# Gated linear attention feeding a maxout feed-forward layer: 16-bit transposition of the results, decay sums by TensorE, copies on either engine, and a new written order

## The chip, the core and the metric

The kernel runs on one core of a Trainium2 chip. The metric is device time in microseconds (us) of one execution. A core has five instruction queues that run side by side and meet only through semaphores: TensorE (PE), which multiplies matrices and writes to the accumulator memory PSUM; VectorE (DVE); ScalarE (ACT); GpSimd (POOL); and SyncE (SP), which here only issues DMA transfers. Each queue works strictly in the order in which its instructions were written, so an instruction that waits holds up everything behind it on its engine.

## The reference

The first half is a recurrence per batch and head, with a state matrix of 48 by 48; the second is a feed-forward layer over all 3072 tokens.

```python
# q, k, v, alpha: (4 batches, 8 heads, 768 steps, 48), alpha in 0.8 to 1.0
for t in range(S):
    state = alpha[:, :, t, :, None] * state + einsum('bhd,bhe->bhde', k[:, :, t], v[:, :, t])
    y[:, :, t] = einsum('bhd,bhde->bhe', q[:, :, t], state)
x = y.transpose(0, 2, 1, 3).reshape(3072, 384)
h = maximum(maximum(x @ w1, x @ w2), x @ w3)      # 384 -> 768
out = h @ w_out                                    # 768 -> 384
```

## The kernel before

**Tiling.** Time is cut into three chunks of 256 steps per batch, which makes twelve chunks n = 0 to 11 (chunk n is time block n // 4 of batch n % 4). A partition holds two neighbouring steps of a chunk, called r = 0 and r = 1, and 64 partitions make one half i of the chunk. The heads go in two groups of four, so a chunk has two units u = 2n and 2n + 1.

**Attention, per chunk.** `decay` takes logarithms of alpha on ACT (L355) and of the product of two neighbours (L350 for the product, on POOL or DVE; L360 for the logarithm). In `prep`, PE sums the logarithms with a triangular matrix (L425) to get the decay of the odd step, and DVE subtracts one logarithm from that, in PSUM, to get the even step (L429, step "L0"). ACT takes both exponentials (L434, tiles `ep` and `en`), and q and k are multiplied with them on POOL or DVE (L439, tile `qk`). PE turns q and k (L464, step "tp"), always two units together from chunk 2 on; DVE copies the turned q and k out of PSUM (L478, tile `qkT`, 128 x 1024 of 16 bits); PE forms the scores (L490, step "A"); DVE masks them (L498, tile `LA`). `state` sums k and v of the chunk (L522, step "pp") and carries the state on (L399, L411). `output` adds the part of the old state (L555) and the masked scores times v (L577) in PSUM. The result is scaled to 16 bits (tile `xb`, L258 on ACT or L260 on DVE), turned on PE into token order (L598, step "xp"), and copied out (L254, tile `xT`).

The turning is a matmul with `order`, a 0/1 matrix that puts the even steps and the odd ones back in sequence; it writes 32-bit numbers:

```python
live[xk] = bank(xk, [P, NFT, P], FP32)
for ft in range(NFT):
    nc.tensor.matmul(live[xk][:, ft, :], xb[:, :, ft], order, start=True, stop=True)
```

**Feed-forward, per chunk.** The maximum of three products is written with differences: w2 - w1 and w3 - w1 are formed once by DVE in place (L307, tile `wcat`, two halves g = 0, 1 of three column pieces each). Six groups of six matmuls per chunk give the two hidden products (L621, step "gp"); the first half passes a ReLU (L630 on ACT, L632 on DVE), the second a maximum with the first (L637, DVE). What w1 does by itself is folded into one matrix `past` = w1 times w_out (L320 transposes w1, L254 copies it to `w1T`, L333 multiplies). An output block of 128 tokens then takes three matmuls with `past` (L654) and six with w_out (L657); ACT or DVE copies it (L254, tile `ob`) and SP stores it (L673).

**Order.** Nothing is scheduled when the kernel is built. Every piece of work is a step with a number; the text `ORDER` lists all step numbers in program order, each with the letter of the engine that runs it (P, V, A, G, S for PE, DVE, ACT, POOL, SP) and the PSUM banks that it takes. For example `28P0` is step 28 on PE in bank 0. So ORDER fixes each engine's queue, the choice of engine where a step may run on two, and the bank each result lies in. There are eight banks. SP issues all loads of q, k, v and alpha (L273), five chunks deep, and the stores; POOL issues the four weight loads (L287, L290), which therefore stand in POOL's queue between its products.

The functions that the change touches, and what calls them:

Of the kernel before, what the change touches and what calls it, by code (L numbers as in the profile page):

```python
# [10 lines left out]
FP32 = mybir.dt.float32  # L11
FP16 = mybir.dt.float16
# [14 lines left out]
0S 3S 53S 6S 7S 5S 2S 1S 11V 12A 8V 13A 4S 10A 28P0 9A 54S 14P1 29V 17P2 57V 55S 30A 18V 31A 56S  # L27
59A 33V 100S 58A 60P3 75P4 19A 102S 63P5 76V 34A 101S 32V 61A 20A 103S 64V 35P6 15A 22V 145S 21V
207S 23A 36V 24P2 148S 65A 16V 40P01 146S 25V 77A 78A 147S 67G 26P6 41V 66A 275S 37P2 39G 79V 343S
42V 209S 38V 80G 208S 277S 74G 82P4 68V 69A 278S 70P2 62G 86G 210S 83V 45P0 276S 71V 81G 27V 104G  # L30
72P4 87P23 73V 46P6 50A 89V 84P4 47A 88V 85V 106A 92P7 48P0 105A 411S 49V 93P2 51P6 94V 97A 110P4
90V 98P5 111V 117P0 107P7 44V 197P2 108A 91V 52A 195P7 189V 112A 95P3 99A 118V 257P6 113A 190V 120A
261P5 258V 96A 196A 191V 325P4 122V 262A 265P3 43V 115G 119A 199P6 266A 329P7 131G 326A 121V 200A
114V 194V 124P0 116A 193V 333P5 125V 123A 330A 128V 126P3 149G 334A 132P67 127V 129P0 150A 331P5
109G 151A 198A 134V 335P3 133V 130V 162P4 137P6 267P2 163V 152P0 263P1 332V 165A 153A 192V 164A
138P5 154G 336V 259P0 211G 139A 136V 155P4 205P3 156V 213A 168G 142V 157A 203P5 161A 135V 260V 158A
166G 220P6 212A 327P7 264V 204A 143P4 268V 159G 214P0 140P1 144A 201P5 221V 141A 167V 215A 206A
227P2 393P4 160V 202A 217G 228V 169P0 279G 328V 229A 176P35 230A 173V 269P7 219G 223A 178V 347G
281A 170V 394A 177V 222A 282P2 174P0 180V 283A 225G 171P3 270A 337P6 175V 280A 232G 611S 172V 345S
288P2 181P7 224G 338A 295P0 272P1 348A 296V 231G 289V 297A 179V 349A 182P6 285V 298A 287V 234P3  # L40
291A 216V 273V 286G 340P5 183A 218G 238V 186A 274S 300G 290A 235V 344S 363P0 239P6 677S 341A 233G
364V 397P1 294A 240V 346S 226G 187P2 479S 350P3 299G 398A 399P4 545S 351A 236P5 188A 293G 400V 414S
241P71 301A 184P3 342S 401P2 242V 185A 284G 243V 413S 237V 366A 403P4 245G 402A 412S 244G 356P7
465P3 292G 480S 247V 309P25 357V 481S 466A 467P6 404V 415G 365A 548S 246V 249P3 359A 248P4 339S
310V 302P0 358A 368G 468V 546S 417A 250P 311V 416A 482S 469P7 353G 306V 313G 251A 271S 312G 461P6
303V 254A 614S 360G 470A 315V 418P2 307P3 547S 314V 462A 304P0 252P7 308V 367G 419A 255P5 463P6
253A 256A 361G 316P2 305V 317P7 362A 395P3 369G 471P4 464V 421G 352G 431P5 318P 355G 472V 354G
370P0 322A 423G 535P6 374V 319A 483G 424P4 527P7 396V 536A 549G 531P2 371V 528A 377P36 425V 430G
551A 375P0 408P7 378V 532A 379V 380G 432V 485A 381G 376V 434A 426A 533P3 436G 433A 382V 492P2 427A
372P0 383V 422G 552P5 484A 320P4 476P6 429G 493V 534V 495A 428G 321A 373V 494A 537P3 477A 435G  # L50
323P4 616A 529P2 409V 324A 538V 385P6 553A 558P0 384P1 550A 486P7 438P4 530V 487A 386P 489G 488V
437G 559V 499P3 565P7 387A 473P2 420V 390V 497G 561A 500V 439V 615G 501A 388P1 405P6 474A 566V 389A
442V 502A 491V 560A 391P2 504G 440P4 392A 593P1 441V 555G 490G 597P3 594A 445P02 568A 443P4 598A
659P1 447V 446V 617A 449G 444V 599P3 406A 496G 407S 663P0 681V 475S 661P6 664A 563V 678S 539P4 660A
498G 600V 410S 683A 564G 612S 567A 448V 618P5 679S 562G 665P0 450V 540V 680S 667P1 451V 505G 541S
666V 631P3 452P7 668A 595P4 613S 632V 619A 503V 624P2 634A 453P0 684P1 513P5 596V 621G 633A 570G
454P 685A 682A 515V 506P3 662V 458A 571G 669P1 455A 625V 635G 514V 627A 459P0 601P6 507V 626A 569G
460A 456P7 670V 542P5 602A 510V 554G 557G 628G 511P0 543A 508P2 579P6 512V 457A 630G 544S 572P4
556G 725P7 516V 509V 687G 729P0 629G 726A 603P1 730A 689G 580V 518P7 731P2 517V 581V 636G 690P3
573V 674P0 691V 582G 576V 637G 519P6 732V 583G 638P4 675A 693A 604V 520P 676S 697P0 622V 727P2 521A  # L60
524V 692A 733P1 698V 639V 699A 522P7 605P6 523A 728V 701G 734A 642V 688G 577P2 606A 574P4 585P7
578V 700A 607S 525P1 671P6 702G 526A 478S 575V 623G 584P0 703G 735P1 672A 696A 694G 673S 586P 736V
645P2 620G 643P3 686G 640P5 646V 608P1 647V 587V 641V 751P2 609A 644V 590A 740P0 610S 591P5 743P6
592V 588P1 649V 747P7 589A 648V 752V 741A 650P3 651P4 765P5 742S 695V 652P 744V 704P0 653A 711P2
656A 769P6 712V 766A 713V 657P3 705V 654P4 715G 770A 737P2 708V 658A 748A 714V 655A 706P5 709P0
717P3 707V 779P7 749P4 780A 710V 787P5 716P6 750V 763P7 718P 753P0 745P1 754V 789P4 719V 761P0 746V
783P6 722V 762A 767P1 764V 723P3 755P0 724V 738V 784V 720P7 758P3 721V 797P2 759V 771P6 788V 760S
805P7 756V 772V 785P3 757S 798V 739S 801P5 806V 781P0 768V 803P6 802V 773P2 790V 804V 799P7 782V
807P1 786V 776P5 800V 808V 791P4 774V 777V 775S 778S 813P6 792V 809P0 793S 817P3 814P 810P 815V
818P 794P7 811A 816S 812S 819V 820S 795A 796S  # L70
# [44 lines left out]
def kernel(  # L115
# [41 lines left out]
    c16_np = np.concatenate([np.kron(both, trimid), halves], axis=1).astype(np.float16)  # L157
# [9 lines left out]
    c16 = sb.tile([P, P + 4], FP16, name="c16")  # L167
    d16 = sb.tile([P, 4 * P], FP16, name="d16")
    c32 = sb.tile([P, 3], FP32, name="c32")
    tri, hsel = c16[:, :P], c16[:, P:]  # L170
# [79 lines left out]
    TB = 2  # L250
    WAFTER = {2: (0,), 4: (1,), 7: (2,), 11: (3,)}
# [164 lines left out]
    def prep(u):  # L416
# [6 lines left out]
        def cums(eng):  # L423
            live[Lk] = bank(Lk, [P, HH, 2, D], FP32)
            nc.tensor.matmul(live[Lk][:, :, 1, :], tri, la[:, 0, hs, :D], start=True, stop=True)  # L425

        plan.step("Lp", "PE", u, cums, banks=[Lk], reads=[("la", n % 3, hh, 0)], writes=[Lk])
        plan.step("L0", "DVE", u,
                  lambda eng: nc.vector.tensor_sub(live[Lk][:, :, 0, :], live[Lk][:, :, 1, :],  # L429
                                                   la[:, 1, hs, :D]),  # L430
                  reads=[Lk, ("la", n % 3, hh, 1)], writes=[(Lk, 0)])
# [39 lines left out]
        for v in units:  # L471
            attend(v, tk)


    def attend(u, tk):
        qkT, LA, Ak = qkTs[u % NT_], LAs[u % NT_], ("A", u)
        plan.step("qkT", "DVE", u,
                  lambda eng: nc.vector.tensor_copy(  # L478
                      out=qkT.rearrange("p i w j t -> p i (w j t)"), in_=live["tp", u]),
                  reads=[tk], writes=[("qkT", u % NT_)])  # L480

        def scores(eng):
            live[Ak] = banks2(Ak, FP32)
# [246 lines left out]
```

## Time and profile before

| | us |
|---|---|
| median of 3 runs | 152.37 |
| lowest and highest of them | 151.62, 154.77 |
| the profiled execution | 150.92 |
| its span, from first to last instruction | 149.2 |
| PE busy, matmuls | 130.2 |
| DVE busy | 121.8 |
| ACT busy | 80.7 |
| POOL busy | 71.8 |

The busy times are sums over the whole span, and a matmul's busy time has a modelled end, so they tell which engine is much used and not yet which one sets the end. For that the profile has the span in 40 slices with the tenths that each engine was busy, and the chain of work that ended last, followed back from the last instruction. A group's row gives line, engine, operation, tiles, shape and count, then busy time and mean duration of one in ns, then how long the engine stood idle just before it and what ended that. Durations of one matmul (200 to 330 ns) are longer than the distance at which they follow each other; the distances come from the timeline.

Input loads keep the DMA near 260 GB/s in the first 78 us; the granted clock of PE was full throughout.

### The profile page before, as it was taken

Reading aid. Unit: us, or ns where it says so; the run is one execution under the profiler, and the core shown is the slowest. Engines: PE = TensorE matmul, PEld = TensorE weight load, DVE = VectorE, ACT = ScalarE, POOL = GpSimd, SP = SyncE. Lnnn points to the kernel's source line nnn. Section 1 sums busy time; section 2 is a strip of 40 time slices with the busy share of each in tenths; the row PEclk is TensorE's granted clock in tenths of the full one; section 3 lists DMA queues with packets and bytes.
Section 4 is the critical chain, followed back from the end, with each engine's and each line's share of the span. In section 5 each row is a group of like instructions: output and inputs, shape, how many; then the busy total and the mean of one; then the engine's idle time right before and its main releaser. Section 6 shows DMA issues by size and latency. Waiting matters only on the chain.

```text
span 149.2 us, 5617 instructions
## 1 busy us (share of the span) xinstructions
PE 130.2 (87%) x2389; PEld 101.2 (68%) x2389; DVE 121.8 (82%) x231; ACT 80.7 (54%) x182; POOL 71.8 (48%) x114
## 2 busy tenths in 40 slices
PE   0136587689999999999999999999999999999991
PEld 0025475468676678887687879778678788787670
DVE  6489996789999979998896899699698785889720
ACT  3565156687896887957877759328522720100011
POOL 8105900430959897999977577994730100000000
PEclk9999999999999999999999999999999999999999
DMA  5999999999999999999996199701211100031223
GB/s 112 266 262 263 252 216 213 278 234 252 277 260 265 258 266 281 254 253 280 276 256 166 57 258 284 203 2 59 105 57 53 57 4 0 4 110 48 81 101 134
DMA packets 54728, 26.34 MB, mean 177 GB/s; under 512 B 50736, under 2 KB 54320, under 8 KB 54704
## 3 DMA queue, kind: packets, MB, share of 16 engines
q1 hardware_dynamic: 53584, 23.60, 63.3%
q0 software_dynamic: 832, 2.36, 8.1%
q8 instruction: 18, 0.29, 0.9%
q10 hardware_dynamic: 288, 0.04, 0.3%
q14 instruction: 6, 0.05, 0.1%
HBM read 23.63 MB, written 4.72 MB: 190 GB/s over the span
## 4 chain that ended last, share of the span: by engine, by line
PE 65%; DMA 10%; POOL 6%; DVE 5%; ACT 4%; SPq 4%; issue 3%; POOLq 0%; DVEq 0%
PE psum L621 26%; PE psum L657 15%; PE psum L654 8%; DMA wcat<-in_moe_w_dram 6%; SPq L273 4%; DMA qn<-in_q_dram 4%; POOL qk L439 3%; PE psum L490 3%; PE psum L577 3%; PE psum L464 3%; PE psum L598 2%; PE psum L333 2%; PE psum L555 2%; PE psum L522 2%; POOL Z L399 1%
## 5 line engine op out<-in xcount | busy, mean ns | idle before, releaser
L621 PE MATMUL psum<-xT,wcat 128*128 128x256 f16 x432 | 54.3, 273 | 2.1 <-DVE wcat L307 2.1
L621 PEld LDWEIGHTS <-wcat 128*128 128x128 f16 x432 | 39.9, 98 | 8.4 <-DVE wcat L307 2.8
L498 DVE TENSOR_TENSOR LA<-psum,d 128x1024 f16<-128x1024 f32 x24 | 28.7, 1217 | 3.7 <-PE psum L490 2.8
L657 PE MATMUL psum<-wo,hT 128*128 128x384 f16 (+1 forms) x150 | 27.5, 320 | 0.0
L637 DVE TENSOR_TENSOR hT<-psum,hT 128x512 f16<-128x512 f32 x36 | 23.7, 680 | 2.9 <-PE psum L621 2.6
L439 POOL TENSOR_TENSOR qk<-qn,ep 128x384 f16<-128x384 f32 x18 | 18.3, 1026 | 11.4 <-DMA qn<-in_q_dram 8.6
L630 ACT ACTIVATE hT<-psum 128x512 f16<-128x512 f32 x28 | 16.4, 601 | 13.6 <-PE psum L621 13.2
L254 ACT COPY ob<-psum 128x384 f32<-128x384 f32 x14 | 6.7, 481 | 27.9 <-PE psum L657 27.9
L657 PEld LDWEIGHTS <-hT 128*128 128x128 f16 x150 | 14.5, 98 | 8.9
L439 POOL TENSOR_TENSOR qk<-kn,en 128x384 f16<-128x384 f32 x16 | 15.9, 998 | 9.4 <-ACT en L434 8.9
L478 DVE COPY qkT<-psum 128x1024 f16<-128x1024 f16 x24 | 16.0, 683 | 1.3 <-PE psum L464 1.1
L654 PE MATMUL psum<-past,xT 128*128 128x384 f16 (+1 forms) x75 | 15.9, 321 | 0.0
L258 ACT ACTIVATE xb<-psum,c 128x384 f16<-128x384 f32 x17 | 9.2, 581 | 8.7 <-PE psum L577 8.6
L434 ACT ACTIVATE en<-psum 128x384 f32<-128x384 f32 x24 | 11.5, 492 | 2.0 <-DVE psum L429 2.0
L464 PE MATMUL psum<-d,qk 64*128 64x64 f16 x384 | 8.8, 198 | 4.1 <-POOL qk L439 2.1
L434 ACT ACTIVATE ep<-psum 128x384 f32<-128x384 f32 x24 | 11.6, 492 | 0.9 <-DVE psum L429 0.6
L254 ACT CAST xT<-psum 128x384 f16<-128x384 f32 x20 | 9.4, 482 | 3.0 <-PE psum L598 2.7
L350 POOL TENSOR_TENSOR aa<-an 128x384 f32<-128x384 f32 x9 | 8.9, 998 | 4.3 <-DMA an<-in_alpha_dram 4.1
L425 PE MATMUL psum<-la,c 128*128 128x192 f16 x24 | 6.1, 272 | 5.5 <-ACT la L360 5.5
L464 PEld LDWEIGHTS <-qk 64*128 64x128 f16 x384 | 7.1, 99 | 5.5 <-DVE qk L439 2.6
L399 POOL TENSOR_TENSOR Z<-U,G 48x192 f16<-48x192 f32 x10 | 5.0, 502 | 11.8 <-DVE U L411 11.5
L490 PE MATMUL psum<-qkT 48*64 48x128 f16 x384 | 9.7, 235 | 0.9 <-DVE qkT L478 0.5
(58 smaller groups left out, 193.7 us busy)
## 6 DMA issues: line engine op xcount, KB each, us to landing
out_dram<-ob SPq DMA_DIRECT2D x23, 192.0 KB, 2.0
an<-in_alpha_dram SPq DMA_DIRECT2D x11, 384.0 KB, 6.3
qn<-in_q_dram SPq DMA_DIRECT2D x11, 384.0 KB, 5.5
kn<-in_k_dram SPq DMA_DIRECT2D x11, 384.0 KB, 6.1
vn<-in_v_dram SPq DMA_DIRECT2D x11, 384.0 KB, 6.3
wcat<-in_moe_w_dram POOLq DMA_DIRECT2D x2, 576.0 KB, 10.1
w1s<-in_moe_w_dram POOLq DMA_DIRECT2D x1, 576.0 KB, 7.7
wo<-in_moe_w_out_dram POOLq DMA_DIRECT2D x1, 576.0 KB, 7.7
```

The costliest lines, as they stand in the source:

```text
L254: (nc.scalar.copy if eng == "ACT" else nc.vector.tensor_copy)(out=out, in_=in_)
L434: lambda eng, t=t, sign=sign: nc.scalar.activation(out=t, in_=live[Lk], func=AFT.Exp, scale=sign),
L439: lambda eng, w=w, x=x, e=e: on[eng].tensor_mul(qk[:, w, :, :, :D].rearrange("p r h d -> p h r d"), ld[x][n % NL][:, hs], e),
L464: nc.tensor.transpose(live["tp", v][:, i, at:at + HALF], qks[v % NQ][rows, w, r, 2 * j:2 * j + 2, :], ident[rows, rows])
L478: lambda eng: nc.vector.tensor_copy(out=qkT.rearrange("p i w j t -> p i (w j t)"), in_=live["tp", u]),
L490: nc.tensor.matmul(live[Ak][i * HALF:(i + 1) * HALF, p, at:at + P], qkT[rows, i, 1, j, r * HALF:(r + 1) * HALF], qkT[rows, i, 0, j, :], st ...
L498: lambda eng: nc.vector.tensor_mul(LA.rearrange("p a j r t -> p (a j) (r t)"), live[Ak].rearrange("p a (j t) -> p (a j) t", j=2), maskA.un ...
L621: nc.tensor.matmul(live[gk][:, jj, :], hidden(wcat[:, g, kt], 2 * j + jj), xT[:, kt, :], start=(kt == 0), stop=(kt == NFT - 1))
L630: nc.scalar.activation(out=h, in_=live[gk], func=AFT.Relu)
L637: lambda eng, h=h, gk=gk: nc.vector.tensor_max(h, live[gk], h),
L654: nc.tensor.matmul(live[ok], xT[:, kt, i * P:(i + 1) * P], past[:, kt, cols], start=(kt == 0), stop=False)
L657: nc.tensor.matmul(live[ok], hT[:, kt, i * P:(i + 1) * P], wo16[:, kt, cols], start=False, stop=(kt == NJ - 1))
```

## The change

1. `output`: the turning becomes a transposition with `order` in the place of the identity, and its result in PSUM has 16 bits.
2. `prep`: for chunks 0 to 2 the even step's decay is made by PE as well, as the triangular sum minus the identity times one logarithm, two more matmuls a unit; the DVE subtraction stays for the later chunks. The constants get a negative identity.
3. `attend`: the copy of turned q and k may run on DVE or ACT (`copy` is the helper that takes either).
4. ORDER is a new one throughout: other sequence, other engines, other banks. Step numbers differ as six subtractions are gone (820 becomes 814 for the last step).

```diff
+    EARLY = 3
...
-    c16_np = np.concatenate([np.kron(both, trimid), halves], axis=1).astype(np.float16)
+    c16_np = np.concatenate([np.kron(both, trimid), -np.eye(P), halves], axis=1).astype(np.float16)
...
-    tri, hsel = c16[:, :P], c16[:, P:]
+    tri, minus, hsel = c16[:, :P], c16[:, P:2 * P], c16[:, 2 * P:]
...
         def cums(eng):
             live[Lk] = bank(Lk, [P, HH, 2, D], FP32)
-            nc.tensor.matmul(live[Lk][:, :, 1, :], tri, la[:, 0, hs, :D], start=True, stop=True)
-
-        plan.step("Lp", "PE", u, cums, banks=[Lk], reads=[("la", n % 3, hh, 0)], writes=[Lk])
-        plan.step("L0", "DVE", u, ...)
+            if n < EARLY:
+                nc.tensor.matmul(live[Lk][:, :, 0, :], tri, la[:, 0, hs, :D], start=True,
+                                 stop=False, skip_group_check=True)
+                nc.tensor.matmul(live[Lk][:, :, 0, :], minus, la[:, 1, hs, :D], start=False,
+                                 stop=True, skip_group_check=True)
+            nc.tensor.matmul(live[Lk][:, :, 1, :], tri, la[:, 0, hs, :D], start=n >= EARLY,
+                             stop=True, skip_group_check=True)
+
+        plan.step("Lp", "PE", u, cums, banks=[Lk], writes=[Lk],
+                  reads=[("la", n % 3, hh, r) for r in range(1 + (n < EARLY))])
+        if n >= EARLY:
+            plan.step("L0", "DVE", u, ...)
...
-        plan.step("qkT", "DVE", u,
-                  lambda eng: nc.vector.tensor_copy(
-                      out=qkT.rearrange("p i w j t -> p i (w j t)"), in_=live["tp", u]),
+        plan.step("qkT", "DVE ACT", u,
+                  lambda eng: copy(eng, qkT.rearrange("p i w j t -> p i (w j t)"),
+                                   live["tp", u]),
                   reads=[tk], writes=[("qkT", u % NT_)])
...
             def turn(eng, xb=xb, xk=xk):
-                live[xk] = bank(xk, [P, NFT, P], FP32)
+                live[xk] = bank(xk, [P, NFT, P], FP16)
                 for ft in range(NFT):
-                    nc.tensor.matmul(live[xk][:, ft, :], xb[:, :, ft], order,
-                                     start=True, stop=True)
+                    nc.tensor.transpose(live[xk][:, ft, :], xb[:, :, ft], order)
```

Of the new order, the beginnings of two queues, which the prediction follows. POOL before: product (u2, q), load w1s, product (u3, k), load of wcat's first half, G, load of its second half. POOL now: products (u1, q), (u1, k), G, product (u3, q), G, load w1s, load of wcat's first half, v scaling, product of chunk 2's alpha, load of wcat's second half. Six of the loads that SP issues first, before: alpha, alpha, alpha of chunk 1, k, v, q of the second heads; now: alpha, alpha, alpha of chunk 1, k of the second heads, k and q of the first heads. The differences (L307) stood, before, one each ahead of the first three groups of L621; now two stand ahead of the first group and the third behind it, and of the second half's three the last stands behind that half's first group. How many steps run where, before and now: copies qkT on DVE 24 and 14, on ACT 0 and 10; copies xT on DVE 4 and 10, on ACT 20 and 14; q/k products on DVE 14 and 19, on POOL 34 and 29; copies `ob` on ACT 14 and 12 of full width.

97 lines of the change are left out of this document (48 added, 49 removed).

## Prediction

> **What bounds the kernel now.** I read the page's 40 slices first, to see where TensorE (PE) is not full; then the engines by stage; then the chain that ended last, through the stage where PE has holes; then the groups by shape for prices.
>
> ```profile
> PE   0136587689999999999999999999999999999991
> DVE  6489996789999979998896899699698785889720
> ```
> A slice is 3.73 us. From the tenth slice on (33 us) PE stands at 9; the holes are in the first nine. So there are two stages: up to about 34 us PE waits for others, behind it PE's own queue sets the end.
>
> The engines by stage (columns: stretch, its length, busy time of each engine, granted clock, DMA share, GB/s):
> ```profile
> 10.00:15.00 5.00, 2.85 (x98) 2.23 (x92) 4.69 (x10) 2.13 (x5) 2.13 (x3) 1.00 1.27 264
> 15.00:20.00 5.00, 3.13 (x108) 2.70 (x109) 4.93 (x6) 0.83 (x2) 3.76 (x6) 1.00 1.17 241
> ...
> 35.00:40.00 5.00, 4.97 (x76) 3.93 (x75) 4.75 (x10) 3.29 (x9) 2.50 (x4) 1.00 1.09 259
> ```
> From 10 to 20 us VectorE (DVE) is busy 9.62 of 10, ScalarE (ACT) 2.96: DVE paces the ramp, while loads fill the DMA at some 262 KB per us.
>
> The chain that ended last, in order of time (start, us, what):
> ```profile
> 12.83 1.40 POOL qk L439
> 14.23 0.73 issue
> 14.96 0.79 POOL qk L439
> 15.90 9.03 DMA wcat<-in_moe_w_dram
> 24.98 0.46 issue
> 25.44 0.57 DVE wcat L307
> 26.05 0.84 PE psum L621 x6
> 26.92 0.57 DVE wcat L307
> 27.54 0.84 PE psum L621 x6
> 28.40 0.57 DVE wcat L307
> ```
> The first feed-forward matmuls (L621) start at 26.05, not when DVE is free but when a weight load lands that POOL could issue only behind two of its q/k products; then subtraction (L307) and matmul take turns, and PE idles 0.65 and 0.54 us. That alternation comes from program order: a difference written behind a matmul group of the same half of wcat waits for that group, and the next group for the difference.
>
> Behind 34.35 us I add up PE's queue by its spacing in the timeline (six L621 in 0.655 us, nine of an output block in 1.46, 32 of L464, L490, L577 in 0.57, 0.57, 0.51). All steps come to 121.2 us, 12.6 of them done by 34.35, so 108.6 are left; PE ends at 145.88, 111.5 us later. Only 2.9 us of stalls are left in that stage.
>
> **The parts.** The prices:
> ```profile
> L478 DVE COPY qkT<-psum 128x1024 f16<-128x1024 f16 x24 | 16.0, 683 | 1.3 <-PE psum L464 1.1
> L425 PE MATMUL psum<-la,c 128*128 128x192 f16 x24 | 6.1, 272 | 5.5 <-ACT la L360 5.5
> L429 DVE TENSOR_TENSOR psum<-psum,la 128x192 f32<-128x192 f32 x24 | 8.5, 357 | 2.0 <-PE psum L425 1.2 <-ACT la L355 0.6
> L598 PE MATMUL psum<-d,xb 128*128 128x128 f16 x72 | 8.2, 231 | 0.3 <-ACT xb L258 0.2
> L254 ACT COPY w1T<-psum 128x768 f16<-128x768 f16 x3 | 2.4, 816 | 0.0
> L254 DVE CAST xT<-psum 128x384 f16<-128x384 f32 x4 | 2.2, 554 | 0.8 <-PE psum L598 0.8
> L320 PE MATMUL psum<-d,w1s 128*128 128x128 f16 x18 | 1.6, 245 | 0.0
> ```
> *Decay sums of chunks 0 to 2 by PE.* Six DVE subtractions go (6 x 0.357 = 2.1 us), twelve 192-column matmuls come, 0.08 us each in a stream (chain: 0.08 per L425), 1.0 us. All stand before 25 us, where PE has holes (2.85 busy of 5), so I cost them at nothing; without that cover they cost 1.0.
>
> *Turn by 16-bit transposition.* 72 matmuls become 72 transpositions of the same shape. L598 streams three in 0.17 us. The nearest transposition, L320, runs six in 0.34 us at 30.2 us, and twelve in 0.92 when it first appears: 57 to 77 ns. I take 57, the row met with PE full: no cost; the other end is 72 x 20 ns = 1.4 us. The copy out then reads f16. For DVE: copies of f32 cost 358 and 552 ns for 192 and 384 columns, fixed part 164; the f16 copy of 1024 costs 683, so 0.51 ns a column and 0.36 us for 384, against 0.554 (bounds 0.26, by pure proportion, and 0.554). ACT: 816 for 768, 482 for 384, no gain.
>
> *qkT copies on either engine.* Ten of 24 go to ACT, by the w1T slope 0.87 ns a column: 1.04 us each there against 0.683 on DVE. The new order moves more: six xT copies and five q/k products to DVE, the latter from POOL. Over the kernel, by rows: DVE some 6 us less, ACT 8.5 more (81 to 89 of 149), POOL 5 less, PE 1.0 more.
>
> *The ramp in the new order.* Before the first difference DVE had 18.4 us of work (32 steps: 5 subtractions 1.8, 6 products 3.4 plus 0.9 of stretching beside POOL, 4 qkT 2.6, 4 LA 4.8, the rest small); now 22 steps with 13.2. That freedom is not a shift of 5 us, since other things come late:
> - ACT must take the logs of chunk 1 (load landed at 6.78) ahead of the first exponentials: 7.9 instead of 6.3. Covered: q of the first half is now sixth of the loads, 1344 KB down the queue, and the sixth landed at 9.03 (DVE waited for it). First transpositions 10.15 against 9.64.
> - The other half's products go to POOL: q lands near 9.8, two products of 1.03 with stretching end near 12.3; so its scores start near 13 and the first LA near 13.6, as in the old trace (13.80). The four LA end near 22.
> - POOL issues w1s and wcat's first half behind three products and two G: near 13.3 and 14.0, against 14.19 and 15.90. The old loads landed 3.0 us apart, so the second lands near 24.0, not 24.9. wcat's second half now stands behind a v scaling and the product of chunk 2's alpha, 18.8 against 16.66; its differences come at 30 us, and it landed 11.2 us after issue: 30.0, hidden by a hair.
> - xT of the first block is behind w1T's copy (0.82) on ACT: near 25.4. So the first L621 starts at 25.4, not 26.05.
> - Two differences are then done and the third waits for the first matmul group: one hole of 0.65 in place of 0.65 and 0.54. Six groups run to 30.4, transposition to 31.0, then a group of the second half; its last difference again waits for that group: a new hole of 0.65, with the qkT copy queued behind it on DVE.
>
> At 34.4 us PE has then done nine L621 groups instead of six and one 0.085 L425, but not the 0.43 of the chunk's sums (L522): 3 x 0.655 + 0.085 - 0.43 - 0.1 (later by that) = 1.5 us ahead.
>
> *Behind 34 us.* Nothing leaves PE's queue, so that lead arrives at the end if no new wait forms. Between a transposition and the scores that need an ACT copy PE has 1.9, 3.3, 3.4, 3.9, 4.0, 6.0 and 6.3 us of other work; the copy needs 1.04 plus about one ACT operation ahead of it (0.5). Between xp and the groups that need its copy the least is 1.3 (1.0 before). So 0 is taken, bounds -2.9 (all stalls gone) and +3. The end: before, a 384-column copy (0.48) and a 192 KB store (2.0 us to landing); now two 192-column copies on two engines (0.36) and two 96 KB stores (1.7), one behind the other on SP: 0.2 saved.
>
> **Sum.** 150.92 (span 149.2 and 1.7 around it) - 1.5 - 0.2 = 149.2. The median of the runs shown, 152.37, is 1.45 above the profiled execution; on its scale the same 1.7 gives 150.7, my forecast.
>
> **Rivals.**
> - *The DVE relief counts in full.* For: 9.62 of 10 busy, 5 us taken off. Against: the weight load and q's landing are not DVE's. If the four LA end 2 us earlier and the holes of 0.65 close too, 1.3 + 1.5 + 1.2 = 4.0: 148.4.
> - *No gain.* wcat lands no earlier since it shares the DMA with loads that also run at 262 KB per us, and the two holes of 0.65 eat the rest; the 1.0 of added matmuls may show: 152.4 to 153.4. For: DMA is full throughout the ramp.
> - *Slower: ACT's queue.* ACT works in order; a 1.04 us copy stands behind exponentials and ReLUs, and scores, LA, output and the block's copies hang on it. It decides when three or more operations (1.6) are ahead, so that 2.7 us beat PE's cover of 1.9 to 6.3. With some 0.9 us for each of the ten, less the 1.7: +7.3, 159.7; with half of them 155.2. Against: ACT is at 8.1 to 8.6 of 10 only between 40 and 80 us.
> - *Slow transpositions.* Were all like L320's first twelve: +1.4, 152.1, the gain gone. L320's second batch and the granted clock of 1.00 in every stretch speak against it. The Trainium skill, TensorE: Matmul & The Clock Gate, Part 4: PE-mode transpose, gives about 275 ns for one in a kernel and says that transposes don't count as activity for the full clock; by that, 72 x (275 - 57) ns would be 15.7 us more, an estimate from that page. The trace disagrees in spacing (57 ns) though not in a single one's duration (245 ns).
>
> **Chances.** Forecast 0.45; DVE relief in full 0.20; no gain 0.19; ACT's queue 0.12; slow transpositions 0.04. A measurement tells some 2% (3.0 us) from no change: faster takes the relief and the forecast's upper edge, 0.26; slower takes ACT's queue and a little of no gain, 0.14; within 2% 0.60. The range runs from the relief (148.4, less 1.2 for stalls that go later) to the upper no gain with half a microsecond of waits, 147.2 to 154.0.
>
> **What would show it.** First L621 at 25 to 25.7; wcat landing near 24; holes near 0.65 behind the first L621 group and behind the first one of the second half; L598's successor at 57 ns spacing; DVE's xT copies near 0.36 us, ACT's qkT near 1.04; PE done near 144.3. Wrong if PE shows waits for ACT's qkT between 40 and 110 us, or if the first L621 comes after 26.5.

## The result and the profile after

The changed kernel takes 152.46 us (median of 17 runs, 151.75 to 155.41) where the kernel before takes 151.62 us (17 runs beside them, 150.83 to 154.77). The ratio is 1.0065, with an interval of 1.004 to 1.009: slower by 0.65%, which is inside the two per cent that count as no change, but on the other side of the forecast, which was 1.1% faster. Ratios here are taken from undisturbed executions of both kernels (in others the kernel before takes 153.3 to 155.2 us), so they can differ from the ratio of two medians. The profiled execution took 152.43 us, its span is 150.4 (before 149.2). These two executions lie 1.5 us apart, where the ratio says 1.0, so some tenths of what the traces show below can be chance of the one execution.

The page's 40 slices of the changed kernel, TensorE (PE) and VectorE (DVE); a slice is 3.76 us:

```profile
PE   0365986879999999899999999999999999999991
DVE  6348893879999799999998987998999851848711
```

PE starts one slice earlier (3, 6, 5, 9, 8 in slices 2 to 6, before 1, 3, 6, 5, 8), is about as weak as before in slices 7 to 9 (6, 8, 7, before 7, 6, 8), and has a new 8 in the seventeenth slice, at 60 us. The stretches of the changed kernel (stretch, length, busy time of PE, PE's weight loads, DVE, ACT and POOL, granted clock, DMA share, GB/s):

```profile
10.00:15.00 5.00, 2.73 (x64) 1.75 (x64) 3.73 (x6) 3.39 (x9) 4.62 (x7) 1.00 1.28 261
15.00:20.00 5.00, 4.03 (x131) 3.31 (x133) 4.48 (x9) 2.55 (x4) 2.13 (x3) 1.00 1.17 239
35.00:40.00 5.00, 4.84 (x87) 3.43 (x84) 4.95 (x9) 3.23 (x8) 0.26 (x1) 1.00 1.02 246
```

From 10 to 20 us DVE is busy 8.21 instead of 9.62, so the relief of the ramp is there; the DMA is as full as before. The chain that ended last, in order of time (start, us, what), through the ramp:

```profile
13.40 0.68 POOL w1s L290
...
14.08 10.64 DMA wcat<-in_moe_w_dram
...
24.81 1.04 DVE wcat L307 x2
...
25.90 0.84 PE psum L628 x6
...
26.77 0.56 DVE wcat L307
...
30.37 1.76 DVE wcat L307 x2
...
32.18 0.73 PE psum L628 x5
...
32.93 0.56 DVE wcat L307
```

The weight load is issued at 14.08 instead of 15.90, and lands at 24.72 instead of 24.93: it now takes 10.64 us, before 9.03. The first feed-forward group starts at 25.90 instead of 26.05.

One thing said ahead of the prediction has to be set right here: TensorE did not run at full speed throughout. In the kernel before, the transpositions of w1 (L320) start up to 107 ns apart from 23.96 to 24.38 us, and 56 ns apart from 24.48 on; the trace's first record of the granted clock, 1.0, stands at 24.45. Ahead of that record the page prints full clock although PE runs at half. In the changed kernel the first record is at 23.06. Both have full speed before the first feed-forward group, so this does not touch the comparison of the two behind it, but it bears on three of the experiments.

The groups by shape that carry the parts of the change (busy time, mean ns | idle before, and what ended it):

```profile
L254 ACT COPY qkT<-psum 128x1024 f16<-128x1024 f16 x10 | 10.1, 1014 | 1.4 <-PE psum L472 1.2
L254 DVE COPY qkT<-psum 128x1024 f16<-128x1024 f16 x14 | 9.5, 684 | 2.5 <-ACT qkT L254 1.3 <-PE psum L472 1.1
L606 PE MATMUL psum<-d,xb 128*128 128x128 f16 x72 | 7.2, 223 | 0.1
L437 DVE TENSOR_TENSOR psum<-psum,la 128x192 f32<-128x192 f32 x18 | 6.4, 358 | 1.4 <-PE psum L430 1.3
L254 DVE COPY xT<-psum 128x384 f16<-128x384 f16 x10 | 3.5, 352 | 5.0 <-ACT ob L254 3.1 <-PE psum L606 1.8
```

The prices came as forecast. What is new stands at the end of the second row: ahead of its copies of turned q and k, DVE was idle 1.3 us waiting for *ACT's* copies.

**Where the time went.** I added up PE's queue again, each matmul at the spacing of its kind, and set apart what lies above it. By 34 us the changed kernel has done 9.78 us of such work against 7.74; 0.98 of it are the added decay sums, so it is 1.06 us ahead. Behind 34 us it loses more than that:

| above the pure spacing, 34 us to the end, us | before | after |
|---|---|---|
| at a change from one kind of matmul to another | 6.14 | 7.43 |
| of this, at the end of a block of scores | 1.54 (13 blocks) | 2.30 (19 blocks) |
| holes of more than 160 ns above the spacing, 0.13 us of each left out | 0.60 (7 holes) | 1.50 (5 holes) |
| inside the blocks | 11.4 | 11.6 |

1.3 + 0.9 + 0.2 are 2.4 us lost against 1.06 won; the last matmul starts at 146.84 instead of 145.54. What counts as pure spacing is a choice: with others the same sum gives 2.1 to 2.2 us, so the parts are good to some 0.3 us.

*The score blocks.* The kernel before, TensorE's timeline (start, us, operation):

```profile
62.16 0.64 PE L490 MATMUL psum<-qkT 48*64 48x128 f16 x32
62.73 0.62 PE L598 MATMUL psum<-d,xb 128*128 128x128 f16 x6
```

and the changed kernel's:

```profile
63.93 0.42 PE L498 MATMUL psum<-qkT 48*64 48x128 f16 x16
64.28 0.83 PE L628 MATMUL psum<-xT,wcat 128*128 128x256 f16 x6
```

The scores of two units in one go take 0.57 us to the start of the next matmul, those of one unit 0.35: two separate blocks cost 0.13 us more than a double one. The loss is at the end: behind the last score a matmul of the whole array starts 148 or 149 ns later in all 15 places of the changed kernel, whereas the sums of L530, which use the same 64-row and 64-column tiles, start 19 to 46 ns later (4 places). The Trainium skill, TensorEngine Tiling (Array Packing), Key Properties, says that a change of tiling mode, not of the tile alone, drains TensorE. The trace agrees with it: wherever neighbours in the queue use the same tiling, the next one follows at the usual spacing, and wherever the tiling changes, it comes later, by 113 ns on average. Counted in this way, without holes, there are 57 changes of tiling behind 34 us instead of 52, which is some 0.5 us of the 1.3; the six more score blocks by themselves overstate it, since other changes have gone. The rest of the 1.3 is not broken down here.

*The holes.* Between 34 and 130 us the kernel before shows no wait of PE of more than 150 ns; the changed one (what waited <- for whom: us, times, longest) has

```profile
PE psum L498 <- DVE qkT L254: 0.7, 2, 0.6
PE psum L370 <- ACT la L360: 0.3, 1, 0.3
PE psum L563 <- DVE Z L399: 0.2, 1, 0.2
```

The longest stands at 60 us. Its timeline, ACT, DVE and PE:

```profile
59.33 1.01 ACT L254 COPY qkT<-psum 128x1024 f16<-128x1024 f16 x1 [0.35 <-PE psum L472]
...
60.37 0.69 DVE L254 COPY qkT<-psum 128x1024 f16<-128x1024 f16 x1 [0.49 <-ACT qkT L254]
...
59.22 0.83 PE L628 MATMUL psum<-xT,wcat 128*128 128x256 f16 x6
59.98 0.58 PE L585 MATMUL psum<-v,LA 64*128 64x48 f16 x32
61.12 0.42 PE L498 MATMUL psum<-qkT 48*64 48x128 f16 x16 [0.56 <-DVE qkT L254]
```

Both units of a chunk are turned into the same two PSUM banks, and the copies of the two on two engines read them only one after the other: DVE's copy starts 0.03 us after ACT's has ended. In six chunks that are turned together one copy is on ACT and one on DVE. In three of them (at 45, 60 and 92 us) the later copy starts 0.03 us after the end of the earlier; in the other three it comes 0.2 to 1.3 us after it, behind other work of its engine; in none do the two overlap. In chunk 1, whose units are turned separately, they do: DVE copies from 16.16 to 16.84, ACT from 16.23 to 17.22. At 60 us PE had 1.2 us of other work behind the turning and the two copies in series take 1.7.

### The profile page after: what moved, and what is told of

Its sections match the earlier page's. It is cut to its first block, busy times and chain, and to the rows that moved or that the text cites. A ratio compares the mean times of both kernels' runs of the same rounds, so it can differ in the third digit from the quotient of the medians.

```text
span 150.4 us, 5650 instructions
## 1 busy us (share of the span) xinstructions
PE 132.5 (88%) x2401; PEld 102.4 (68%) x2401; DVE 117.1 (78%) x224; ACT 88.7 (59%) x188; POOL 68.2 (45%) x109
## 4 chain that ended last, share of the span: by engine, by line
PE 55%; DVE 19%; DMA 10%; ACT 4%; issue 4%; POOL 3%; SPq 3%; DVEq 0%; POOLq 0%
PE psum L628 22%; PE psum L664 13%; DMA wcat<-in_moe_w_dram 7%; PE psum L661 7%; DVE LA L506 4%; DVE hT L644 3%; DMA qn<-in_q_dram 3%; PE psum L498 3%; SPq L273 3%; DVE qkT L254 3%; DVE wcat L307 3%; DVE qk L447 2%; PE psum L606 2%; POOL qk L447 2%; PE psum L472 2%
## 5 line engine op out<-in xcount | busy, mean ns | idle before, releaser
L637 ACT ACTIVATE hT<-psum 128x512 f16<-128x512 f32 x30 | 17.2, 604 | 15.3 <-PE psum L628 15.1
L447 POOL TENSOR_TENSOR qk<-kn,en 128x384 f16<-128x384 f32 x15 | 15.0, 998 | 12.2 <-DMA kn<-in_k_dram 9.2
L447 POOL TENSOR_TENSOR qk<-qn,ep 128x384 f16<-128x384 f32 x14 | 14.2, 1023 | 13.1 <-DMA qn<-in_q_dram 10.7
L399 POOL TENSOR_TENSOR Z<-U,G 48x192 f16<-48x192 f32 x15 | 7.7, 511 | 15.4 <-DVE U L411 12.0
L254 ACT COPY ob<-psum 128x384 f32<-128x384 f32 (+1 forms) x13 | 6.1, 472 | 13.6 <-PE psum L664 12.4
L254 DVE COPY qkT<-psum 128x1024 f16<-128x1024 f16 x14 | 9.5, 684 | 2.5 <-ACT qkT L254 1.3
L498 PE MATMUL psum<-qkT 48*64 48x128 f16 x384 | 10.2, 235 | 1.3 <-DVE qkT L254 0.7
L254 DVE COPY ob<-psum 128x384 f32<-128x384 f32 (+1 forms) x12 | 6.4, 537 | 6.1 <-PE psum L664 6.1
L254 ACT COPY qkT<-psum 128x1024 f16<-128x1024 f16 x10 | 10.1, 1014 | 1.4 <-PE psum L472 1.2
L260 POOL TENSOR_SCALAR v<-vn,c 128x384 f16<-128x384 f32 x13 | 8.7, 671 | 2.3 <-DMA vn<-in_v_dram 2.1
```

Of the source, the lines that this page charges most:

```text
L254: (nc.scalar.copy if eng == "ACT" else nc.vector.tensor_copy)(out=out, in_=in_)
L447: lambda eng, w=w, x=x, e=e: on[eng].tensor_mul(qk[:, w, :, :, :D].rearrange("p r h d -> p h r d"), ld[x][n % NL][:, hs], e),
L498: nc.tensor.matmul(live[Ak][i * HALF:(i + 1) * HALF, p, at:at + P], qkT[rows, i, 1, j, r * HALF:(r + 1) * HALF], qkT[rows, i, 0, j, :], st ...
L637: nc.scalar.activation(out=h, in_=live[gk], func=AFT.Relu)
```

## The experiments

Two theories were tested first: that the split pairs of copies ate up the gain (**copies in series**), and that one of the other edits did (the turn, the decay sums, the place of the differences). A kernel whose name begins with a_ is an edit of the changed kernel, with b_ of the kernel before; all ratios are to the kernel before, so the mark to compare an a_ kernel with is 1.0065. Numbers in ORDER are those of the kernel that is edited.

### The turn's form

`a_t32`: the changed kernel with the old matmul; `b_t16`: the kernel before with the transposition.

```diff
-                live[xk] = bank(xk, [P, NFT, P], FP16)
+                live[xk] = bank(xk, [P, NFT, P], FP32)
-                    nc.tensor.transpose(live[xk][:, ft, :], xb[:, :, ft], order)
+                    nc.tensor.matmul(live[xk][:, ft, :], xb[:, :, ft], order, ...)
```

> The changed kernel with the turning done as before, a matmul into 32 bits; order and engines as changed. Theory: PE's work is the same (both stream at 56 ns), DVE's ten xT copies take 0.554 instead of 0.352 us, 2.0 us more of DVE off the critical path: 0 to +0.6 us against the changed kernel, ratio 1.006 to 1.011. Rival, slow transpositions: 72 of them cost up to 20 ns more each than matmuls, and the time falls by up to 1.4 us, ratio 0.997 to 1.004.

> The kernel before with one part of the change: the turning by transposition into 16 bits, in the old order. Theory: 72 transpositions stream as the matmuls did, four DVE copies take 0.35 instead of 0.554 us: no change within 0.4 us, ratio 0.997 to 1.003. Rival, slow transpositions: up to 20 ns each, 1.4 us, ratio 1.005 to 1.010.

Measured: a_t32 1.0072 (1.0032 to 1.0113), b_t16 1.0024 (0.9966 to 1.0083). The form of the turn neither costs nor gains anything that can be measured, in either order. The rival of slow transpositions has fallen: they follow each other at 56 ns and last 223. Of the Trainium skill's section on this, TensorE: Matmul & The Clock Gate, Part 4: PE-mode transpose, neither the 275 ns nor the missing full clock shows here: they last 223 ns, and 56 ns is the distance at full speed.

### The decay sums

`a_noearly`: DVE subtracts for chunks 0 to 2 again, at the place of the sums; `b_early`: PE makes them in the old order, DVE's step is left empty.

```diff
-            if n < EARLY:
-                nc.tensor.matmul(live[Lk][:, :, 0, :], tri, la[:, 0, hs, :D], start=True, ...)
-                nc.tensor.matmul(live[Lk][:, :, 0, :], minus, la[:, 1, hs, :D], start=False, ...)
-            nc.tensor.matmul(live[Lk][:, :, 1, :], tri, la[:, 0, hs, :D], start=n >= EARLY, ...)
+            nc.tensor.matmul(live[Lk][:, :, 1, :], tri, la[:, 0, hs, :D], start=True, stop=True)
+            if n < EARLY:
+                nc.vector.tensor_sub(live[Lk][:, :, 0, :], live[Lk][:, :, 1, :], la[:, 1, hs, :D])
```

> The changed kernel with the decay of the even steps of chunks 0 to 2 by a DVE subtraction, as before, at the place of the sums; twelve matmuls less, six subtractions more. Theory: the matmuls lie in PE's holes and cost nothing, the subtractions (0.357 each) lengthen the ramp a little in front of a weight load that sets its end anyway: 0 to +0.6 us, ratio 1.006 to 1.011. Rival: the 1.0 us of added PE work shows, and the time falls by 0.5 to 1.0, ratio 1.000 to 1.004.

> The kernel before with one part: the even decay of chunks 0 to 2 by two more matmuls a unit, no DVE subtraction there, in the old order. Theory: DVE paces the ramp of the old order (9.6 of 10 us busy from 10 to 20), but a weight load ends it; five subtractions (1.8 us) leave ahead of that load, so the first feed-forward group moves by 0.5 at most: -0.6 to +0.2, ratio 0.996 to 1.001. Rival: the twelve matmuls (1.0 us) show: ratio 1.003 to 1.007.

Measured: a_noearly 1.0263 (1.0209 to 1.0317), b_early 1.0027 (0.998 to 1.0074). In the old order the added matmuls cost nothing that can be measured, and the saved DVE time buys nothing, since the weight load lands at 24.89, before at 24.93. In the new order, taking the same edit out costs some 3 us. The timeline of a_noearly, PE and then DVE:

```profile
27.07 0.94 PE L624 MATMUL psum<-xT,wcat 128*128 128x256 f16 x7 [1.39 <-DVE wcat L307]
...
23.40 0.37 DVE L427 TENSOR_TENSOR psum<-psum,la 128x192 f32<-128x192 f32 x1 [0.74 <-PE psum L425]
...
25.72 0.37 DVE L427 TENSOR_TENSOR psum<-psum,la 128x192 f32<-128x192 f32 x1 [0.76 <-PE psum L425]
26.00 1.01 DVE L307 TENSOR_TENSOR wcat<-wcat,w1s 128x768 f16<-128x768 f16 x2
```

Each subtraction stands idle 0.75 us for PE in DVE's queue, the two differences behind them start at 26.00 instead of 24.81, and the first group at 27.07 instead of 25.90. So 1.2 of the 3 us are lost ahead of the first group. Most of the rest is speed, as the page's row of the granted clock shows (tenths, 40 slices):

```profile
PEclk9999999789999999999999999999999999999999
```

From 28.66 to 32.07 us PE had half its clock: 23 matmuls that follow each other at 109 ns elsewhere took 4.2 us instead of 2.5, 1.7 lost. PE had been idle 1.39 and 0.55 us just before; that this idle time took the clock away is likely and not shown. So the 3 us are not the price of six subtractions. They were put where the sums stood; with a better place they might cost less, which was not tried.

### The copies in series

`a_dve`: the six ACT copies whose partner is on DVE go back to DVE. `b_split`: the same six units' copies on ACT in the old order. `a_un2`: only two of them go back.

```diff
 a_dve                                        b_split
-122A 167A 232A 297A 433A 501A               -128V 173V 238V 303V 439V 507V
+122V 167V 232V 297V 433V 501V               +128A 173A 238A 303A 439A 507A
 a_un2
-167A 297A
+167V 297V
```

> The changed kernel, but the six qkT copies that share a turned pair with a copy on the other engine are back on DVE (units 5, 7, 9, 10, 14, 16), nothing else changed. Theory, split pairs: the two copies of a pair read the same two PSUM banks and run one after the other (DVE's copy at 60.37 starts when ACT's ends at 60.34), so a pair takes 1.01 + 0.69 us on two engines instead of 0.69 + 0.61 on one, and holds both queues; PE's holes behind it at 45.5, 60.4 and 94 us (0.51, 0.74, 0.34) go, and the time falls by 0.7 to 1.6 us against the changed kernel, to a ratio of 0.996 to 1.002 against the kernel before. Rival, relief: ACT's copies are worth having since DVE is the fuller engine; with 4.1 us back on DVE the time rises by 0.5 to 2 us, ratio 1.010 to 1.020.

> The kernel before with one part: the qkT copies of units 5, 7, 9, 10, 14 and 16 on ACT, one of each turned pair, in the old order. Theory, split pairs: each pair's second copy waits for the first on the other engine, 0.4 us and a stalled queue each, and ACT's copy takes 1.01 us: +0.8 to +3 us, ratio 1.005 to 1.020. Rival, relief: DVE has 4.1 us less and the time falls or stays, ratio 0.990 to 1.002.

> The changed kernel with two of the ten copies of turned q and k back on DVE, the two of units 7 and 10, behind which TensorE stood at 45.5 us (0.51, the sums of logarithms wait for ACT's logarithm behind the copy) and at 60.4 us (0.74, the scores of unit 11 wait for DVE's copy behind ACT's). If these two stalls are part of what the new order lost, 1.2 us less than the changed kernel: ratio to the kernel before 0.995 to 1.001. If the time goes to other stalls once DVE has the copies, as with all six put back: 1.004 to 1.012.

Measured: a_dve 1.0103 (1.0041 to 1.0166), b_split 1.0204 (1.0137 to 1.0271), a_un2 1.011 (1.0045 to 1.0174). In the old order splitting pairs costs 2%, as the theory of the copies in series wants it; the group of DVE's copies shows the waits. (PE was at half speed until 33.44 us in the traced execution of b_split, so how the 2% is made up can't be read from it.)

```profile
L254 DVE COPY qkT<-psum 128x1024 f16<-128x1024 f16 x18 | 12.2, 686 | 4.8 <-ACT qkT L254 2.7 <-PE psum L464 2.0
```

But taking the split out of the new order does not give the time back. PE's waits in a_un2, 34 to 130 us:

```profile
PE psum L499 <- DVE LA L507: 0.9, 1, 0.9
PE psum L499 <- DVE qkT L255: 0.7, 2, 0.6
PE psum L662 <- DVE V L412: 0.4, 1, 0.4
```

Its timeline at 60 us, DVE and PE:

```profile
59.17 1.21 DVE L507 TENSOR_TENSOR LA<-psum,d 128x1024 f16<-128x1024 f32 x1
60.30 1.27 DVE L255 COPY qkT<-psum 128x1024 f16<-128x1024 f16 x2
...
61.63 0.42 PE L499 MATMUL psum<-qkT 48*64 48x128 f16 x16 [0.57 <-DVE qkT L255]
```

The hole at 60 us is the same 0.57 as with the copy on ACT: DVE is at a masked copy (L507) until 60.30 and then makes both copies one behind the other. The one at 45 us moves by 1.4 us and becomes a wait for DVE's state update, and a new one of 0.9 appears near 102 us. So the copies in series are what PE waits for at 60 us, but undoing them is no cure: the place in the order leaves 1.2 us between turning and scores, and neither way of making two copies fits.

### The place of the differences

`a_dfirst`: in the new order the third difference of each half also stands ahead of the first group that reads the half. `b_dfirst`: in the old order all three of a half do.

```diff
 a_dfirst: 185V moved ahead of 255P0, 186V ahead of 261P7
 b_dfirst: 190V and 191V moved ahead of 257P6, 192V ahead of 331P5
```

> The changed kernel with the third difference of each wcat half moved ahead of the first matmul group that reads this half, so that no difference stands between two groups. Theory: of the holes at 26.6 and 32.7 us (0.71 each) the wait of difference for group and group for difference goes; the first group then starts one difference (0.5) later each time, so 0.2 each, 0.2 to 0.8 us in all if everything behind follows: ratio 1.001 to 1.005. Rival, the holes don't count because DVE's queue sets the pace there (differences were stretched to 0.92 us beside POOL): no change, 1.005 to 1.009.

> The kernel before with the three differences of a wcat half written together ahead of the first matmul group that reads this half. Theory: the holes at 26.6 and 28.2 us (0.82 and 0.71 over the spacing) go, the first group starts two differences (1.0) later, since it then waits for all three: -0.2 to -0.6 us, ratio 0.996 to 0.999. Rival, the groups' results and DVE's queue set the pace there: no change, 0.999 to 1.003.

Measured: a_dfirst 1.0053 (1.0023 to 1.0084), no different from the changed kernel; b_dfirst 1.0202 (1.0158 to 1.0245). Moving the differences closes the holes behind the first groups and gives nothing: the groups start later instead, in the second half of a_dfirst with 1.32 us of idle time ahead of them in place of 0.55 and 0.54. The 2% of b_dfirst are another matter. Its chain:

```profile
26.17 1.35 DVE wcat L307 x2
27.51 0.05 issue
27.56 5.09 PE psum L621 x23
32.65 0.60 PE psum L320 x6
```

Those 23 matmuls start 213 ns apart, not 109: PE had half its clock until 33.09 us, the first record of the granted clock in this trace (before: 24.45). They took 4.9 us where 2.5 were enough, and L320's second transpositions came at 32.44 instead of 30.23; at full speed they would have come at about 30.1, so the moved differences by themselves neither gained nor lost. Why the clock came later is not shown. PE stood idle 0.49 us ahead of the first group and 1.34 us within it; but 153.68 to 154.73 us, what the six executions of b_dfirst took, is a time that the kernel before also takes without the edit. So the 2% can't be put down to the edit.

### The score blocks

`b_asep`: in the old order six double blocks of scores are pulled apart. `a_apair`, `a_apdve`, `b_apair`: blocks joined, by moving the first unit's scores (and their masked copy) down to the second's, where needed into other banks, in a_apdve with the copies of a_dve.

```diff
 b_asep, one of six                     a_apair, one of eight
-174P0 171P3 270A 337P6                 -120P3 ... 149P1 329P5 ... 121V 123P6
+174P0 270A 337P6 171P3                 +149P1 329P5 ... 120P3 123P6 ... 121V
```

> The kernel before with six neighbouring score pairs pulled apart: the second unit's scores one PE step later. Theory of 0.145 us a block: 0.9 us more, ratio 1.003 to 1.009, score blocks behind 34 us 19 or 20 in place of 13. Rival 'no cost of its own': 0.998 to 1.002.

> The changed kernel with the scores of the two units of a chunk made neighbours in PE's queue in eight places where other matmuls stood between them (the first unit's scores are moved down to the second's). Theory 'each separate block of 64-row-tile scores costs PE 0.145 us at its end': eight blocks fewer, some 1.0 us less than the changed kernel, ratio to the kernel before 0.997 to 1.002, and the number of score blocks behind 34 us falls from 19 to some 11 with the same loss per block. Rival 'the place of the scores does not matter, the waits do': the later scores make the masked copies on DVE later and the ratio stays at 1.006 or rises to 1.02, with more holes above 160 ns.

> The same, and in addition the six copies of turned q and k that had gone to ACT while the partner unit's copy is on DVE go back to DVE. If the lost time behind 34 us is made up of score blocks (1.0 us) and of copies in series (0.9 us of holes), both are gone: 0.988 to 0.998. If putting copies back on DVE only moves the holes, as it did without the joined scores (1.010), 1.000 to 1.012.

> The kernel before with four separated score pairs joined in the same way. Theory of 0.145 us a block: 0.6 us less, ratio 0.995 to 0.999. Rival (place does not matter, or the later masked copies cost more): 1.000 to 1.015.

Measured: b_asep 1.0025 (0.9947 to 1.0102); the others 1.073, 1.0739 and 1.0415. In b_asep the loss at the ends of score blocks behind 34 us is 2.63 us instead of 1.54. Counted as in the table there are 23 blocks instead of 13, but one of them has only come behind the mark, as this execution's ramp was longer, and some are pieces of one block among sums of the same tiling. Ends that cost 147 to 150 ns to the next start are 17 instead of 10, which makes 1.0 of the 1.1 us. Whether the median moves by that much the interval doesn't tell. The three joined kernels tell nothing about it: a block of scores takes two neighbouring banks, and at five of the eight places (three of the four in b_apair) one of them still held another result. There a part of the scores or of that result is overwritten, and steps that had nothing to do with each other wait on the shared bank (11.2 us of holes in a_apair), so their times are no price of a block. A joining in free banks was not run.

### The weight load

`a_w`: POOL issues w1s and the first half of wcat ahead of its third product. `a_wun2`: with the two copies of a_un2 as well.

```diff
-75G ... 60G 37G 71G
+37G 71G 75G ... 60G
```

> The changed kernel with POOL's two loads (w1s, first half of wcat) issued ahead of its third product instead of behind it and a small operation, about 1.0 us earlier. The prediction's step 'landing follows the issue at the spacing of the old loads' gives wcat's landing at 23.7 in place of 24.7, the first feed-forward group near 25.4 (then the first turned block binds) and a ratio of 1.000 to 1.004. The rival 'the loads share the DMA, which is full, so they land when it has moved what was issued before them' gives a landing at 24.4 to 24.8 and 1.004 to 1.012, the product that now stands behind the loads being 1.3 us later.

> Both edits together. If both losses are what they seem, 0.992 to 0.999 and faster than either kernel; if stalls only move, 1.003 to 1.015.

Measured: a_w 1.006 (1.0018 to 1.0102), a_wun2 1.0137 (1.0085 to 1.0188). The load's place does move its landing. In a_wun2 it is issued at 13.22 and lands 10.8 us later, at 24.0, and the first group starts at 25.39 instead of 25.90. But something else lands later. POOL's timeline, the changed kernel:

```profile
17.28 1.00 POOL L350 TENSOR_TENSOR aa<-an 128x384 f32<-128x384 f32 x1 [1.59 <-DMA an<-in_alpha_dram]
18.23 0.60 POOL L290 DMA_DIRECT2D wcat<-in_moe_w_dram  x1
```

and a_wun2's:

```profile
20.63 0.99 POOL L351 TENSOR_TENSOR aa<-an 128x384 f32<-128x384 f32 x1 [4.49 <-DMA an<-in_alpha_dram]
21.56 0.60 POOL L291 DMA_DIRECT2D wcat<-in_moe_w_dram  x1
```

Moving two loads of 576 KB up by 0.9 us delayed the next chunk's alpha by 3.35 us, and with it the load of wcat's second half, which POOL issues behind that product. Here DMA time was exchanged, not won.

### DVE's load behind 34 us

Over the whole span DVE has 4.7 us less to do than before (117.1 against 121.8). But not everywhere. From 35 to 125 us, the kernel before:

```profile
35.00:125.00 90.00, 89.70 (x1775) 70.44 (x1774) 78.17 (x142) 59.08 (x136) 59.43 (x87) 1.00 0.73 181
```

and the changed kernel:

```profile
35.00:125.00 90.00, 88.73 (x1803) 68.87 (x1801) 81.08 (x151) 61.33 (x133) 52.85 (x78) 1.00 0.74 186
```

DVE has 2.9 us *more* there (third busy time), POOL 6.6 less: the new order has 11 q/k products on DVE behind 34 us, the old one 5. The third theory was that this load makes the holes. `a_pool`: six of the products back to POOL. `a_pooldve`: with the copies of a_dve. `b_prod`: six products put on DVE in the old order.

```diff
 a_pool                                       b_prod
-219V 422V 491V 498V 622V 688V               -225G 292G 299G 428G 497G 628G
+219G 422G 491G 498G 622G 688G               +225V 292V 299V 428V 497V 628V
```

> The changed kernel with six of the eleven q/k products that DVE has behind 34 us given back to POOL, in the same places of the order. Theory 'behind 34 us the new order has more work on DVE than the old one (81.1 us busy of 90 against 78.2, with POOL at 52.9 against 59.4), and that makes the stalls': DVE 3.3 us less, stalls of 1.5 us shrink by 0.5 to 1.3 us, ratio to the kernel before 0.997 to 1.003. Rival 'the products are wanted at once, and POOL takes 1.00 us for one where DVE takes 0.55': 1.006 to 1.015.

> The same, and the six copies of turned q and k whose partner is on DVE go back to DVE, so that DVE has 0.8 us more than in the changed kernel and no copy waits for one on another engine. If the copies in series cost time by themselves as in the old order (where splitting six pairs cost 3 us): 0.990 to 1.002. If DVE's load alone decides: 1.005 to 1.012.

> The kernel before with six q/k products behind 34 us moved from POOL to DVE, as the new order has them: 3.3 us more on DVE. If DVE's load in that stage is what binds: 1.004 to 1.015, with stalls of the scores and sums behind DVE's copies. If DVE has room there (13.0 of 15 busy): 0.997 to 1.003.

Measured: a_pool 1.0061 (1.0021 to 1.0101), a_pooldve 1.0087 (1.005 to 1.0125), b_prod 1.047 (1.0409 to 1.053). In a_pool DVE is down to 78.95 us in that stretch, nearly the old figure, and the holes behind 34 us, counted as in the table, are 1.69 us against 1.50: the same five places, and one more. Nothing supports the theory for the new order. In the old order the same move costs 7 us, more than either theory allowed. The last section shows the largest piece in its trace, a wait of PE of 2.37 us; behind it, from 64.35 to 67.76 us, PE had half its clock, which cost some 1.5 us more:

```profile
PEclk9999999999999999779999999999999999999999
```

## Why the prediction was wrong, point by point

- *Prices of the parts*: right. 56 ns between the transpositions (57 taken), 0.352 us for DVE's xT copy (0.36), 1.014 for ACT's qkT copy (1.04), nothing that can be measured on PE for the decay sums (b_early). But the 77 ns of L320's first twelve were no price of a transposition: they are gaps of up to 107 ns at half speed and of 56 at full, so the granted clock, named against *slow transpositions* as 1.00 in every stretch, was misread.
- *"The second lands near 24.0"*: mis-sized. The weight load landed at 24.72. The old spacing was carried over, though the load shares the full DMA with others: landing moved by 0.2 us where issue moved by 1.8. So the first group came at 25.90 instead of 25.4. The rival *no gain* had named the shared DMA, and in a_wun2 the 0.7 us won for this load was taken from another.
- *"One hole of 0.65"* in each half: the first is there (0.54), the second half has two (0.55 and 0.54). Its two differences took 1.76 us instead of 1.1 beside POOL's product of alphas at 30.72.
- *"1.5 us ahead" at 34 us*: 1.06. Mis-sized by the two points above.
- *"Behind 34 us 0 is taken"*: **this is the step that failed.** It was 2.4 us, inside the bounds of -2.9 and +3 but by two mechanisms that the sum had no term for. First, PE's queue was added up by the spacing inside blocks, as if the order of the blocks were free; changes of kind, among them 57 changes of tiling instead of 52, cost 1.3 us more (by the trace; b_asep shows the price at the end of a block too, and leaves its effect on the time open). Second, five holes took 0.9 us more than those before, the largest from copies in series: the cover of 1.9 to 6.3 us was counted "between a transposition and the scores that need an ACT copy"; the partner's copy on DVE, which comes after ACT's, was not in that list, and at 60 us its cover is 1.2 against 1.7. That wait itself is shown; putting the copy back on DVE did not cure it (a_un2). The remaining 0.2 is inside the blocks. All of this is an account of one trace each; no experiment gave the lost time back.
- *DVE "some 6 us less"*: 4.7 over the span, and +2.9 in the stage that PE's queue binds. A sum over the kernel hid where it falls. With it nearly taken back, in a_pool, the time is the same.
- *Decay sums at nothing*: right as a cost. The prediction gave them no worth either, beyond the DVE time: taking them out of the new order costs 3 us (1.2 ahead of the first group, 1.7 by half speed behind it), putting them into the old one gains none. An edit's worth depends on the order around it.
- *The end*: 0.1 us saved, 0.2 taken.
- *Rivals*: the *DVE relief in full* fell, since the ramp ended with a weight load. *No gain* gave 152.4 to 153.4, and on the scale of its median (152.37) the measured ratio is 153.4: through the landing it named, but more through the stage it left out; so its number was met in part by luck. *ACT's queue* is there with a small part of its size: 0.3 us of waits for ACT's logarithm behind a copy.

What stays open: which of the new order's choices makes which of the five holes behind 34 us (38.5, 45.5, 60.4, 94.0 and 114.7 us). Seven edits of the new order (all but a_t32, a_noearly and the two with joined scores) took none of them away without another in its place, and gave 1.005 to 1.014. No version beat the kernel before.

## What to carry to other kernels

Where one engine's queue sets the end, add it up with a price at each change between kinds of work, not only with the spacing inside a block: blocks split by a reordering are new work. When a copy is given to a second engine, ask whether its partner reads the same PSUM banks, and count the cover for the *later* of the two. A lead won in a full DMA can be paid for by another load (a_wun2). And before a loss is put down to waits, look at the distance between matmuls: in b_dfirst, a_noearly and b_prod 1.5 to 2.4 us were lost because TensorE ran at half speed for a while.

## What the runs showed of the hardware

- Behind a block of 48 x 64 tiles a matmul of the whole array starts 148 ns after the last score, one in the same tiling 19 to 46 ns after it.
- TensorE starts at half speed, and can fall back to it. Matmuls of 256 columns then follow each other at 213 ns instead of 109, transpositions of 128 at 107 instead of 56. Full speed came at 24.45 us before, at 23.06 in the changed kernel, at 33.09 in b_dfirst. Four traces have a later stretch of half speed, each 3.41 us long: a_noearly from 28.66, b_prod from 64.35, b_apair from 76.98, and b_t16 from 27.66, whose ratio of 1.0024 is no change; so one traced execution does not say that an edit brings it every time.
- A product on DVE can last four times as long as its 0.55 us. In b_prod, timeline of DVE, POOL and PE:

```profile
59.02 2.37 DVE L439 TENSOR_TENSOR qk<-qn,ep 128x384 f16<-128x384 f32 x1
...
59.03 0.99 POOL L350 TENSOR_TENSOR aa<-an 128x384 f32<-128x384 f32 x1
59.99 0.99 POOL L439 TENSOR_TENSOR qk<-kn,en 128x384 f16<-128x384 f32 x1
...
62.95 0.33 PE L555 MATMUL psum<-Z,qkT 128*128 128x96 f16 x4 [2.37 <-DVE hT L637]
```

  DVE's product ends 0.41 us after the second POOL product, less than the 0.55 it takes alone, so it did little or nothing while POOL's two ran; DVE's work behind it came late, and PE then stood for 2.37 us. The prediction had put this down as 0.9 us of "stretching" for the whole ramp. The Trainium skill, SBUF — State Buffer, section SBUF: two separate sides, says that DVE and GpSimd share a pair of ports as an exclusive lock that is held for a whole instruction, for a DVE operation with two SBUF inputs among others. This trace agrees, as far as one place can: the delay is about as long as POOL's two instructions. Of the six products moved in b_prod, four took longer than 0.55 us (0.68 to 2.37).
